# Token weights turned by DMA transposes instead of TensorE, and a reordered first batch, in a fused attention and token-mixing kernel

## The chip, the cores and the metric

The kernel runs on one core of one Trainium2 chip. The metric is device time in microseconds, the median of several executions.

Engine names in the profile: PE is TensorE's matmuls and PEld its weight loads, DVE is VectorE, ACT is ScalarE, POOL is GpSimd (it issues the loads from memory here) and SP is SyncE (it issues the DMA transposes and the stores).

## The reference, cut to what matters

Four batches, eight heads, 768 tokens, head size 64, so a model width of 512.

```python
# attention: local window of 96 tokens plus 8 global ones, with a slope per head
scores = scale * q @ k.T + bias                      # (4, 8, 768, 768)
a = softmax(where(keep, scores, -1e9));  x = a @ v   # -> (4, 768, 512)
# phase mixing of tokens
theta = x @ w_theta                                  # (512, 512)
zr, zi = x * cos(theta), x * sin(theta)
u = x + w_tok_r @ zr + w_tok_i @ zi                  # w_tok_*: (768, 768), on the token axis
out = u + relu(u @ w_ch)                             # (512, 512)
```

The kernel's token mix takes the token weights with the summed token on the partitions, so both `w_tok` matrices are transposed once: 72 blocks of 128 by 128.

## The kernel before

The four batches are software-pipelined. While batch b is mixed (theta, sines, token mix, channel product), the attention of batch b+1 runs beside it. The first batch's attention has nothing beside it and is ordered by hand.

The loads go through one queue on GpSimd, in the order in which they are issued, and convert float32 to bfloat16 on the way:

```python
    load_w()            # w_theta, six loads of w_tok (two row blocks of one matrix each), w_ch
    load_all_qk(1)      # q and k of batch 1
    load_all_v(1)
    load_all_qk(2)
    ...                 # v of batch 2 and half of batch 3's q, k: later, from the stage's step list
```

The token weights are transposed on TensorE, six blocks at a time, and copied from PSUM:

```python
    def trans_w(tt, copy=nc.vector.tensor_copy):
        for wi in range(2):
            ps = ps_small([T, NT, T], BF)
            for st in range(NT):
                nc.tensor.transpose(ps[:, st, :], w_nat[wi, tt][:, st * T:(st + 1) * T], ident)
            (copy if wi else nc.vector.tensor_copy)(out=w_tokT[wi][:, :, tt * T:(tt + 1) * T], in_=ps)
```

`trans_w(0)` stands in the first batch's tail. The other five are woven into batch 0's mixing stage, one ahead of each token row block.

q and k are transposed on TensorE as well. Two heads share one 128-wide transpose, which needs the heads side by side in memory, so VectorE rearranges first:

```python
    def prep_copy(b, p):                       # rearranging copies, two per pair of heads
        ...
            for i_ in range(2):
                nc.vector.tensor_copy(out=qkn[:, :, i_].rearrange("p t h d -> p h t d"),
                                      in_=qk[:, i_, 2 * p:2 * p + 2])

    def prep(b, p):
        ...
                for t_ in range(NT):
                    nc.tensor.transpose(ps[:, t_, :], qkn[:, t_, i_].rearrange("p h d -> p (h d)"), ident)
```

The first batch's tail, in order of issue:

```python
    values(0, NP - 1, 0)
    values(0, NP - 1, 1)          # last pair of heads, all six token blocks
    trans_w(0, nc.scalar.copy)
    xtrans(0, NP - 1)             # x of the last pair, transposed
    for c in range(NT // 2):      # theta of two token blocks at a time, all four pairs
        theta(0, c, 0)
        theta(0, c, 1)
```

For batches 1 to 3 the transposes of x and u are DMA transposes from SyncE. `prep(1, *)` and `prep(2, *)` both run in batch 0's mixing stage. Batch 3's q and k are transposed by DMA.

The softmax here doesn't subtract the row's maximum and nothing guards it: scores larger than these inputs give would overflow.

Of the kernel before, what the change touches and what calls it, by code (L numbers as in the profile page):

```python
# [9 lines left out]
FP = mybir.dt.float32  # L10
# [6 lines left out]
def kernel(  # L17
# [90 lines left out]
    load_qk(0, 2, 2)  # L108
    load_v(0, 0, 4)
    load_qk(0, 4, 2)  # L110
# [29 lines left out]
    def bias_table(p):  # L140
        for h in (2 * p, 2 * p + 1):
            nc.scalar.activation(etab[:, h], dist[:, 0:5], AF.Exp, scale=-slopes[h])  # L142
# [8 lines left out]
    w_nat = {}  # L151
    w_tokT = [const.tile([T, NT, S], BF, name=f"w_tokT_{wi}") for wi in range(2)]

    def load_w():
        nc.gpsimd.dma_start(out=w_theta_bf, in_=moe_w_theta.rearrange("(c p) n -> p c n", p=T))
        for tt in range(0, NT, 2):
            for wi, src in enumerate((moe_w_tok_r, moe_w_tok_i)):
                w2 = moe.tile([T, 2, S], BF, name="w_nat", bufs=6)
                nc.gpsimd.dma_start(
                    out=w2, in_=src[tt * T:(tt + 2) * T, :].rearrange("(a p) s -> p a s", p=T))  # L160
                w_nat[wi, tt], w_nat[wi, tt + 1] = w2[:, 0], w2[:, 1]
        nc.gpsimd.dma_start(out=w_ch_bf, in_=moe_w_ch.rearrange("(c p) n -> p c n", p=T))

    def trans_w(tt, copy=nc.vector.tensor_copy):
        for wi in range(2):
            ps = ps_small([T, NT, T], BF)
            for st in range(NT):
                nc.tensor.transpose(ps[:, st, :], w_nat[wi, tt][:, st * T:(st + 1) * T], ident)
            (copy if wi else nc.vector.tensor_copy)(out=w_tokT[wi][:, :, tt * T:(tt + 1) * T], in_=ps)


# [21 lines left out]
    def cast0(p, i_, eng, h=None):  # L193
        if (p, "n") not in tiles0:
            tiles0[p, "n"] = att.tile([T, NT, 2, 2, D], BF, name="qkn", bufs=2)
        src = qk32[:, i_] if p == 0 else loads[0][0][:, i_, 2 * p:2 * p + 2]
        hs = slice(0, 2) if h is None else slice(h, h + 1)
        eng(out=tiles0[p, "n"][:, :, i_, hs].rearrange("p t h d -> p h t d"), in_=src[:, hs])

    def turn0(p, i_):  # L200
        qkn = tiles0[p, "n"]
        ps = tiles0[p, i_] = ps_small([T, NT, T], BF)
        for t_ in range(NT):
            nc.tensor.transpose(ps[:, t_, :], qkn[:, t_, i_].rearrange("p h d -> p (h d)"), ident)
# [9 lines left out]
    def kglob(b, p):  # L214
        kT = qkT[(b, p)][1]
        kG = qkT[(b, p)][2] = att.tile([T, NT - 2, T], BF, name="kG", bufs=6)
        with behind("dve") if b == B - 1 else nullcontext():
            nc.vector.tensor_copy(  # L218
                out=kG, in_=kT[:, T:(NT - 1) * T].rearrange("p (t n) -> p t n", t=NT - 2))
            nc.vector.tensor_copy(out=kG[:, :, 0:NG], in_=kT[:, None, 0:NG].to_broadcast([T, NT - 2, NG]))  # L220

    qkns = {}

    def prep_copy(b, p):
        qk = loads[b][0]
        qkn = qkns[b, p] = att.tile([T, NT, 2, 2, D], BF, name="qkn", bufs=2)
        with behind("dve"):
            for i_ in range(2):
                nc.vector.tensor_copy(  # L229
                    out=qkn[:, :, i_].rearrange("p t h d -> p h t d"), in_=qk[:, i_, 2 * p:2 * p + 2])  # L230

    def prep(b, p):
        if p == 0:
            prep_copy(b, 0)
        if p + 1 < NP:
            prep_copy(b, p + 1)
        qkn = qkns[b, p]
        qT = att.tile([T, S], BF, name="qT", bufs=6)
        kT = att.tile([T, S], BF, name="kT", bufs=6)
        for i_, dst in ((0, qT), (1, kT)):  # L240
            ps = ps_small([T, NT, T], BF)
            with behind("pe"):
                for t_ in range(NT):
                    nc.tensor.transpose(ps[:, t_, :], qkn[:, t_, i_].rearrange("p h d -> p (h d)"), ident)  # L244

            dst = dst.rearrange("p (n t) -> p n t", t=NT)
            src = ps.rearrange("p t n -> p n t")
            if i_ == 0:
                nc.vector.tensor_copy(out=dst, in_=src)
            else:  # L250
                nc.scalar.copy(out=dst, in_=src)

        qkT[(b, p)] = [qT, kT, None]
        kglob(b, p)
# [42 lines left out]

    def score_exp(b, p, c):
# [4 lines left out]
        if c == NT // 2 - 1 and p == NP - 1:  # L303

            with tc.issue_after(ins) if b else nullcontext():
                nc.scalar.activation(junk, halfpi, AF.Sin)
# [29 lines left out]
    def values(b, p, hh):  # L336
# [9 lines left out]
        for it in range(NT):  # L346
            mms = [(e_t[:, hh, it, 0, :], vn[:, h, it, :])]
            if it:
                mms.append((e_t[:, hh, it - 1, 1, :], vG[:, h, it - 2, :] if it > 1 else vn[:, h, 0, :]))
            o = po[:, 0, it * (D + 1):(it + 1) * (D + 1)]  # L350
            for i_, (l_, r_) in enumerate(mms):
                nc.tensor.matmul(o, lhsT=l_, rhs=r_, start=(i_ == 0), stop=(i_ == len(mms) - 1))  # L352
# [5 lines left out]
        po4 = po[:, :, 0:NT * (D + 1)].rearrange("p a (t d) -> p a t d", d=D + 1)  # L358
        rec = att.tile([T, n, NT, 1], FP, name="rec", tag=f"rec{n}")
        nc.vector.reciprocal(rec, po4[:, :, :, D:D + 1])  # L360
        xv = x_sb[b][:, p, :, h0 * D:(h0 + n) * D].rearrange("p t (a d) -> p a t d", a=n)
        nc.vector.tensor_mul(xv, po4[:, :, :, 0:D], rec.to_broadcast([T, n, NT, D]))  # L362

    def xtrans(b, p, copy=nc.vector.tensor_copy):
# [6 lines left out]
        for st in range(NT):  # L371
            nc.tensor.transpose(ps[:, st * T:(st + 1) * T], x_sb[b][:, p, st, :], ident)
        copy(out=xT_sb[b][:, p, :], in_=ps)
# [4 lines left out]
    def theta(b, c, j):  # L378
        if c == 0 and j == 0:
            zri[b] = moe.tile([T, 2, NT, DM], BF, name="zri", tag="zri", bufs=1)  # L380
        xT, xb = xT_sb[b], x_sb[b]
        last = c == NT // 2 - 1
        if j == 0:
            pss["th"] = [ps_small([T, DM], FP) for _ in range(2)] if last else ps_big()
        pb = pss["th"]
        st = lambda j_: slice((2 * c + j_) * T, (2 * c + j_ + 1) * T)
        for j_, dc in ([(0, dc) for dc in range(NC - 1)] if j == 0 else
                       [(1, dc) for dc in range(NC - 1)] + [(0, NC - 1), (1, NC - 1)]):
            nc.tensor.matmul(pb[j_] if last else pb[:, j_, :], lhsT=xT[:, dc, st(j_)],  # L389
                             rhs=w_theta_bf[:, dc, :], start=(dc == 0), stop=(dc == NC - 1))  # L390
        if j == 1:
# [11 lines left out]
    def mix(b, tt, g):  # L403
# [3 lines left out]
        for st in (2 * g, 2 * g + 1):  # L407
            for wi in range(2):
                anchor["pe"] = nc.tensor.matmul(  # L409
                    ps, lhsT=w_tokT[wi][:, st, tt * T:(tt + 1) * T], rhs=zri[b][:, wi, st, :],  # L410
# [43 lines left out]
    gate = const.tile([1, 1], BF)  # L454

# [6 lines left out]
    def attention_steps(b, preps):  # L462
# [3 lines left out]
        add(0, alloc_x, b)  # L466
        chunks = [(p, c) for p in range(NP) for c in range(NT // 2)]
# [3 lines left out]
        for i_ in range(0, len(chunks), 2):  # L471
# [3 lines left out]
            if b == B - 1 and i_ in (0, 2, 6):  # L475
                add(0, kglob, b, (1, 2, 0, 3)[i_ // 2])
            if i_ == 8:
# [26 lines left out]
    load_w()  # L504
    load_all_qk(1)
    load_all_v(1)
# [6 lines left out]
    cast0(0, 1, dve, 0)  # L513
    cast0(0, 1, act, 1)
    turn0(0, 1)
    cast0(0, 0, dve, 0)
    cast0(0, 0, act, 1)
    turn0(0, 0)
    out0(0, 1, act, 0)
# [3 lines left out]
    kglob(0, 0)  # L523
    score_bias(0, 0)
    score_bias(0, 1)
    score_mms(0, 0, 0)
    score_mms(0, 0, 1)
    score_exp(0, 0, 0)
    cast0(1, 1, dve)
    cast0(1, 0, dve)  # L530
    diagonals(1)
    turn0(1, 1)
    turn0(1, 0)
    for p in range(NP):
        nxt = p + 1 < NP
        score_exp(0, p, 1)
        if nxt:
            out0(p + 1, 1, act)
            out0(p + 1, 0, dve)
            kglob(0, p + 1)  # L540
# [3 lines left out]
        score_bias(p, 2)  # L544
        score_mms(0, p, 2)
        score_exp(0, p, 2)
        if p + 2 < NP:
            cast0(p + 2, 1, dve)
            cast0(p + 2, 0, dve)
            diagonals(p + 2)  # L550
        if p == 0:
            vglob(0, 0, 4)
        if p == 1:
            vglob(0, 4, 4)
        if nxt:
            score_bias(p + 1, 0)
            score_mms(0, p + 1, 0)
            score_exp(0, p + 1, 0)
            score_bias(p + 1, 1)
            score_mms(0, p + 1, 1)  # L560
            if p + 2 < NP:
                turn0(p + 2, 1)
                turn0(p + 2, 0)
        if p:
            xtrans(0, p - 1, act if p == NP - 1 else dve)
    values(0, NP - 1, 0)
    values(0, NP - 1, 1)
    trans_w(0, nc.scalar.copy)
    xtrans(0, NP - 1)
    for c in range(NT // 2):  # L570
        theta(0, c, 0)
        theta(0, c, 1)
    for p in range(NP):
        bias_table(p)
# [5 lines left out]
    for b in range(B):  # L580
# [4 lines left out]
        ahead = [[lambda p=p: prep(2, p) for p in range(NP)], [lambda p=p: prep_dma(3, p) for p in range(1)],  # L585
# [9 lines left out]
        for tt in range(NT):  # L595
            for g in range(NT // 2):
                if (b, tt) != (B - 1, NT - 1):
                    main.append((2048, lambda tt=tt, g=g: mix(b, tt, g)))
                if b == 0 and g == 1 and tt + 1 < NT:
                    main.append((1536, lambda tt=tt: trans_w(tt + 1)))  # L600
# [59 lines left out]
```

## Time and profile before

175.32 us, median of 3 runs (175.06 to 175.37). The profiled execution spans 172.6 us.

These are rows of the page's second part: the span in 40 slices of 4.3 us, busy tenths for the engines, granted clock, busy share of the 16 DMA engines, and GB/s. The last line is the chain of waits by engine.

```profile
PE   6479979999999999999999998999999989999991
DVE  7678965678999999999587588597786837724443
PEclk9999999999999999999999999999999999999998
DMA  5999999999999999879999997787138571323335
...
PE 59%; DVE 21%; ACT 10%; DMA 6%; issue 1%; SPq 0%; DVEq 0%; ACTq 0%
```

Counting slices from 1, TensorE is full from slice 7 on. The DMA row reads 9 until slice 16, about 70 us. VectorE is full from slice 11 to 19.

Marks from the trace: first exp of the first batch at 9.32 us, its last exp ends at 25.30, first sine at 29.91, first token mix at 33.17. The last product of z ends at 36.45 us for batch 0, 81.31 for batch 1, 116.15 for batch 2 and 149.75 for batch 3. I use these four marks to say in which stage time is lost.

### The profile page before, as it was taken

How to read it: one execution, taken by the hardware profiler on the slowest of the kernel's cores; microseconds unless marked ns; L12 is line 12 of the kernel's file. 1: busy time of each engine (PE TensorE's matmuls, PEld its weight loads, DVE VectorE, ACT ScalarE, POOL GpSimd, SP SyncE). 2: the span in 40 equal slices, each digit the busy share in tenths (PEclk: the TensorE clock that was granted, in tenths of full speed). 3: DMA queues.
4: the chain of work that ended last, by engine and by line, in shares of the span. 5: the costliest groups of instructions: out<-in, count | busy, mean ns of one | idle time of the engine just before them, and what ended most of it. 6: DMA issues, size and time to landing. Idle time of an engine off the chain costs nothing.

```text
span 172.6 us, 3652 instructions
## 1 busy us (share of the span) xinstructions
PE 159.9 (93%) x1482; PEld 83.5 (48%) x1482; DVE 128.5 (74%) x288; ACT 99.1 (57%) x124; POOL 37.9 (22%) x45
## 2 busy tenths in 40 slices
PE   6479979999999999999999998999999989999991
PEld 1245655455756566544455463444554634444440
DVE  7678965678999999999587588597786837724443
ACT  2479676999497595489834740979348308500010
POOL 8974355005272010099300000000000000000000
PEclk9999999999999999999999999999999999999998
DMA  5999999999999999879999997787138571323335
GB/s 146 192 193 178 210 208 209 204 204 171 160 204 175 166 155 128 132 97 154 210 141 80 224 158 165 138 152 226 30 76 113 135 171 40 142 41 102 100 93 182
DMA packets 75088, 25.92 MB, mean 150 GB/s; under 512 B 63168, under 2 KB 72128, under 8 KB 75072
## 3 DMA queue, kind: packets, MB, share of 16 engines
q0 software_dynamic: 45680, 12.45, 78.4%
q1 hardware_dynamic: 28976, 12.72, 36.6%
q10 hardware_dynamic: 416, 0.52, 0.9%
q8 instruction: 11, 0.18, 0.4%
q14 instruction: 5, 0.04, 0.1%
HBM read 25.69 MB, written 6.29 MB: 185 GB/s over the span
## 4 chain that ended last, share of the span: by engine, by line
PE 59%; DVE 21%; ACT 10%; DMA 6%; issue 1%; SPq 0%; DVEq 0%; ACTq 0%
PE ps L409 29%; PE ps L434 10%; PE pb L389 5%; PE pb L295 4%; PE pb L352 4%; DVE x_sb L362 4%; ACT etab L142 3%; PE ps L389 3%; ACT e L302 3%; DMA qk<-in_k_dram 3%; DVE kG L218 2%; DVE e L312 2%; ACT cs L395 2%; DMA kT<-qk 2%; DMA xT<-x_sb 2%; PE ps L244 2%
## 5 line engine op out<-in xcount | busy, mean ns | idle before, releaser
L409 PE MATMUL ps<-zri,w_tokT 128*128 128x512 bf16 x288 | 70.6, 380 | 0.3 <-DVE o_sb L440 0.2
L302 ACT ACTIVATE e<-pb 128x1024 bf16<-128x1024 f32 (+1 forms) x48 | 43.6, 958 | 23.1 <-PE pb L295 22.9
L409 PEld LDWEIGHTS <-w_tokT 128*128 128x128 bf16 x288 | 26.1, 98 | 29.0 <-issue 1.0
L414 DVE TENSOR_TENSOR u<-x_sb,ps 128x512 bf16<-128x512 bf16 x24 | 16.4, 682 | 14.6 <-PE ps L409 14.6
L434 PE MATMUL ps<-w_ch_bf,uT 128*128 128x512 bf16 x96 | 24.2, 379 | 0.0
L398 DVE TENSOR_TENSOR zri<-x_sb,cs 128x512 bf16<-128x512 bf16 x48 | 17.9, 418 | 8.0 <-ACT cs L395 7.8
L440 DVE SCALAR_TENSOR_TENSOR o_sb<-ps,u 128x512 f32<-128x512 f32 (+1 forms) x25 | 16.5, 662 | 3.1 <-PE ps L434 3.1
L395 ACT ACTIVATE cs<-pb,halfpi 128x1024 bf16<-128x1024 f32 x8 | 8.9, 1116 | 15.7 <-PE pb L389 15.7
L312 DVE TENSOR_TENSOR e<-e,etab 128x1024 bf16<-128x1024 bf16 (+1 forms) x24 | 14.7, 615 | 3.4 <-ACT e L302 3.4
L389 PE MATMUL pb<-w_theta_bf,xT 128*128 128x512 bf16 x64 | 15.2, 379 | 1.0 <-DMA xT<-x_sb 1.0
L295 PE MATMUL pb<-qT,kT 64*128 64x128 bf16 x224 | 15.6, 219 | 0.6 <-DVE qT L211 0.3
L295 PEld LDWEIGHTS <-kT 64*128 64x128 bf16 x224 | 9.0, 94 | 14.1 <-issue 12.5
L389 PEld LDWEIGHTS <-xT 128*128 128x128 bf16 x96 | 9.0, 98 | 12.0 <-DMA xT<-x_sb 2.4
L428 ACT COPY uT<-ps 128x512 bf16<-128x512 bf16 x7 | 4.1, 587 | 18.6 <-PE ps L427 18.6
L352 PEld LDWEIGHTS <-e 128*128 128x128 bf16 x352 | 12.7, 97 | 3.3 <-issue 1.5
L434 PEld LDWEIGHTS <-uT 128*128 128x128 bf16 x96 | 8.9, 98 | 10.0 <-ACT uT L428 0.3
L295 PE MATMUL pb<-qT,kG 64*128 64x128 bf16 x128 | 11.7, 217 | 1.2 <-DVE kG L220 1.2
L88 POOL DMA_DIRECT2D vn<-in_v_dram x5 | 9.7, 1930 | 12.2 <-DVE vn L68 10.6
L362 DVE TENSOR_TENSOR x_sb<-pb,rec 128x768 bf16<-128x768 f32 x12 | 11.4, 949 | 0.3
L315 DVE TENSOR_TENSOR e<-e,etab 128x1024 bf16<-128x1024 bf16 x12 | 8.2, 684 | 2.8 <-ACT e L302 2.8
L352 PE MATMUL pb<-vn,e 128*128 128x65 bf16 x168 | 9.6, 193 | 0.3 <-DVE x_sb L362 0.3
L82 POOL DMA_DIRECT2D qk<-in_q_dram x8 | 7.4, 920 | 8.8 <-DVE qkn L229 5.0
(74 smaller groups left out, 203.0 us busy)
## 6 DMA issues: line engine op xcount, KB each, us to landing
out_dram<-o_sb SPq DMA_DIRECT2D x23, 256.0 KB, 2.4
vn<-in_v_dram POOLq DMA_DIRECT2D x3, 768.0 KB, 22.7
qk<-in_q_dram POOLq DMA_DIRECT2D x2, 768.0 KB, 21.0
qk<-in_k_dram POOLq DMA_DIRECT2D x2, 768.0 KB, 23.6
w_nat<-in_moe_w_tok_r_dram POOLq DMA_DIRECT2D x3, 384.0 KB, 13.7
w_nat<-in_moe_w_tok_i_dram POOLq DMA_DIRECT2D x3, 384.0 KB, 14.6
vn<-in_v_dram POOLq DMA_DIRECT2D x2, 384.0 KB, 8.9
qk<-in_q_dram POOLq DMA_DIRECT2D x8, 96.0 KB, 9.7
```

The source lines that it names most:

```text
L295: nc.tensor.matmul(pb[:, hh, o:o + T], lhsT=lhsT, rhs=qT[R, (own, nxt)[part]], start=bool(b), stop=bool(b) or (jt == NT - 1 or (j == 1 and ...
L302: ins = nc.scalar.activation(e_c, pb[:, :, 0:n], AF.Exp, scale=scale).ins
L312: nc.vector.tensor_mul(e_c, e_c, tab[:, :, s0:s0 + n // T].rearrange("p a s n -> p a (s n)"))
L352: nc.tensor.matmul(o, lhsT=l_, rhs=r_, start=(i_ == 0), stop=(i_ == len(mms) - 1))
L362: nc.vector.tensor_mul(xv, po4[:, :, :, 0:D], rec.to_broadcast([T, n, NT, D]))
L389: nc.tensor.matmul(pb[j_] if last else pb[:, j_, :], lhsT=xT[:, dc, st(j_)], rhs=w_theta_bf[:, dc, :], start=(dc == 0), stop=(dc == NC - 1))
L395: nc.scalar.activation(o, p_, AF.Sin, **bias)
L398: nc.vector.tensor_mul(zri[b][:, i_, 2 * c + j_, :].rearrange("p (g d) -> p g d", g=NP), xb[:, :, 2 * c + j_, :], cs[:, i_, j_].rearrange( ...
L409: anchor["pe"] = nc.tensor.matmul(ps, lhsT=w_tokT[wi][:, st, tt * T:(tt + 1) * T], rhs=zri[b][:, wi, st, :], start=(st == 0 and wi == 0), ...
L414: anchor["dve"] = nc.vector.tensor_add(u_sb[b, tt].rearrange("p (g d) -> p g d", g=NP), x_sb[b][:, :, tt, :], ps.rearrange("p (g d) -> p g ...
L434: nc.tensor.matmul(ps_c, lhsT=uT[:, dc, :], rhs=w_ch_bf[:, dc, :], start=(dc == 0), stop=(dc == NC - 1))
L440: nc.vector.scalar_tensor_tensor(o_sb[:, cols], in0=ps_c[:, cols], scalar=0.0, in1=u[:, cols], op0=ALU.max, op1=ALU.add)
```

## The change

The intent is to take work off TensorE and VectorE in the stage where both are busy, and to reach the first theta earlier.

1. Token weights: no `trans_w`. Each load of weights (384 KB) is followed by a DMA transpose from SyncE into `w_tokT`. A gate stands behind each pair of weight loads: a tiny GpSimd copy that reads the pair's second tile, so that the loads issued after it start only when the pair has landed. The order of the loads changes so that keys of batch 1 come before the third pair.
2. Column tiles: q and k are transposed one head at a time, 64 columns wide, into one half of the PSUM tile's partitions. The rearranging copies fall away.
3. First batch: theta of the first three pairs goes ahead of the last pair, which is done in two token pieces. Score biases, bias tables and copies move.
4. Half of batch 2's q and k preparation moves from batch 0's stage into batch 1's.

```diff
+    def after_load(tile):
+        return nc.gpsimd.tensor_copy(out=gate, in_=tile[0:1, 0, 0:1]).ins
+
+    def load_w_tok(tt):
+        for wi, src in enumerate((moe_w_tok_r, moe_w_tok_i)):
+            w2 = moe.tile([T, 2, S], BF, name="w_nat", bufs=6)
+            nc.gpsimd.dma_start(
+                out=w2, in_=src[tt * T:(tt + 2) * T, :].rearrange("(a p) s -> p a s", p=T))
+            nc.sync.dma_start_transpose(
+                out=w_tokT[wi][:, tt:tt + 2].rearrange("p a s t -> p (a s) t"),
+                in_=w2.rearrange("p a s -> p (a s)"))
+        return w2
...
+    def turn(ps, src):
+        for t_ in range(NT):
+            for hh in range(2):
+                nc.tensor.transpose(ps[hh * D:(hh + 1) * D, t_, :], src[:, hh, t_, :], ident)
...
-    def prep_copy(b, p):            # and its calls
...
-    load_w()
+    nc.gpsimd.dma_start(out=w_theta_bf, in_=moe_w_theta.rearrange("(c p) n -> p c n", p=T))
+    after_load(load_w_tok(0))
+    after_load(load_w_tok(2))
     load_all_qk(1)
+    after_load(load_w_tok(4))
+    nc.gpsimd.dma_start(out=w_ch_bf, in_=moe_w_ch.rearrange("(c p) n -> p c n", p=T))
     load_all_v(1)
     load_all_qk(2)
...
-    values(0, NP - 1, 0)
-    values(0, NP - 1, 1)
-    trans_w(0, nc.scalar.copy)
-    xtrans(0, NP - 1)
-    for c in range(NT // 2):
-        theta(0, c, 0)
-        theta(0, c, 1)
+    values(0, p, 0, 0, 4)           # p = NP - 1: last pair, token blocks 0 to 3
+    values(0, p, 1, 0, 4)
+    xtrans(0, p - 1, act)
+    sine_table()
+    theta(0, 0, 2)                  # blocks 0 and 1, first three pairs
+    xtrans(0, p, dve, 0, 4)
+    values(0, p, 0, 4, 6)
+    values(0, p, 1, 4, 6)
+    theta(0, 1, 2)
+    theta(0, 0, 3)                  # blocks 0 and 1, last pair: then its sines
+    xtrans(0, p, dve, 4, 6)
+    theta(0, 1, 3)
+    theta(0, 2, 2)
+    theta(0, 2, 3)
...
-        ahead = [[lambda p=p: prep(2, p) for p in range(NP)], ...
+        ahead = [[lambda p=p: prep(2, p) for p in range(NP // 2)], ...
...
-                if b == 0 and g == 1 and tt + 1 < NT:
-                    main.append((1536, lambda tt=tt: trans_w(tt + 1)))
```

## The prediction

> **What bounds the kernel now.** Span 172.6 us. The chain of waits is 59% TensorE, 21% VectorE, 10% ScalarE. By stage (windows, timeline, chain):
> - 0 to 28 us, attention of the first batch: ScalarE and VectorE in turns; TensorE works about 15 us of it. First exp at 9.32 us, last at 25.3, theta products from 28.15, first sine at 29.91, first token mix at 33.17.
> - 42 to 61 us: VectorE is 99 to 100% busy (7.54 of 7.60 us, 11.0 of 11.0), TensorE's queue follows it. 61 to 80: TensorE again; first mix of batch 1 at 80.36.
> - 80 to 105: TensorE (24.9 of 25.0 us). Afterwards nothing that the change touches.
> - Loads: the DMA row is 9 in every slice to 70 us, at about 206 GB/s. Token weights land at 21.6, 23.4, 25.3, 27.3, 29.1, 31.0 us, keys of batch 1 at 41.3, its values at 48.05. The first transposes of batch 1 start at 41.7, on their heels.
>
> **Removed.** 72 TensorE transposes of token weights, 12 in 0.67 us: 4.0 us, 3.3 of it after 33 us; 11 VectorE copies (0.45 us each on the chain, about 5) and one ScalarE copy. All 22 rearranging copies of q and k (16 of 0.27 us and 6 of 0.3): about 4.5 us of VectorE from 41 us on, 1.8 before.
>
> **Added.** Twice as many q/k transposes, half as wide. The Trainium skill (TensorEngine Tiling, Restrictions and Gotchas) says that column tiling excludes fast weight load, yet may run two tiles at once. Row tiles in this trace do (16 score matmuls in 0.55 us). Estimate: 12 take 0.40 us where 6 took 0.34; at worst 0.67. Plus six DMA transposes of 384 KB. "TRN2 transpose DMAs are as fast as regular DMAs" (Advanced Engine Details and Errata, X-Bar Transpose); here a 192 KB one lands 1.55 us after its issue when alone, but took 8.7 us from its issue beside loads at 57 us. At the best packet rate seen, one of 384 KB is 1.5 us of all engines: 9 us in all. Three gates on the load queue add gaps, which the transposes partly fill.
>
> **Moved.** Half of batch 2's q/k preparation goes from the VectorE-bound stage into the TensorE-bound one: about 1.5 to 2.5 us lost there. Theta of three pairs goes ahead, the last pair in two pieces: first sine near 27 (-3 us).
>
> **On the critical path.** VectorE loses about 11 us of work between 41 and 75 us, so TensorE could finish batch 0's stage 5 to 6 us earlier, if data were there. But keys of batch 1 land no earlier (41 to 43), so the 3 us of the first stage are mostly spent waiting; values of batch 1 slip from 48 to 54 or later, and VectorE's copy of them stands ahead of the score multiplications. I expect half or more of the gain to be given back there.
>
> **Time:** 173.0 us, 167 to 180 eight times in 10. Chances: faster 0.38, same 0.42, slower 0.20.
>
> **What would show it.** Right: first sine near 27 us; no rearranging copies; new TensorE or VectorE waits on a DMA (keys, token weights or values of batch 1) between 34 and 60 us; VectorE below 90% from 42 to 61. Wrong: values of batch 1 landing before 50 us (then 168 to 170), or after 58 (then 178 or more); 12 column-tile transposes above 0.6 us.
>
> **What would make it wrong.** DMA transposes that hardly disturb the loads, or starve beside them; column tiles that do not overlap; late transposes of x for batch 1 behind the longer load queue.

## More of the kernel before

The next lines are busy times by stretch, in us from the span's start. The columns are the stretch and its length, then PE, PEld, DVE, ACT and POOL busy time with instruction counts, then granted clock, the mean DMA share (the time that packets took, over the stretch; it exceeds 1 where their times overlap) and GB/s.

```profile
36.00:42.00 6.00, 5.94 (x44) 2.99 (x42) 4.40 (x11) 5.98 (x9) 2.21 (x1) 1.00 1.68 189
42.00:50.00 8.00, 7.83 (x96) 5.40 (x94) 7.94 (x20) 5.64 (x9) 3.28 (x5) 1.00 2.42 173
50.00:60.00 10.00, 9.56 (x130) 5.37 (x128) 10.00 (x21) 7.26 (x9) 2.46 (x3) 1.00 2.37 177
60.00:68.00 8.00, 7.68 (x116) 5.16 (x115) 8.00 (x19) 6.20 (x8) 0.83 (x1) 1.00 2.13 137
68.00:74.00 6.00, 5.99 (x50) 3.35 (x48) 6.00 (x16) 2.20 (x4) 0.39 (x2) 1.00 1.08 161
74.00:82.00 8.00, 8.00 (x54) 3.79 (x53) 7.67 (x20) 7.80 (x10) 8.00 (x9) 1.00 1.22 110
```

From 36 to 82 us VectorE is busy 44.0 of 46.0 us, and TensorE 45.0. Both are full.

## The result, and the profile after

The changed kernel takes 196.28 us (196.01 to 197.99, 4 runs); the kernel before in the same rounds takes 175.34 (175.06 to 176.01). The ratio is 1.121, with a 95% interval of 1.114 to 1.128. It is slower by 12%, far outside the predicted range.

The same rows of the page, after (slices of 4.9 us, as the span is 194.5 us):

```profile
PE   7589987922964759996999999979999998999991
DVE  5656865511370197895668887748687782843442
PEclk9889999985695766999999999999999999999999
DMA  5999999999999999999999977877824545232424
...
PE 48%; DMA 32%; POOL 7%; DVE 7%; issue 2%; ACT 1%; SPq 1%; DVEq 0%; POOLq 0%; ACTq 0%
```

The chain of waits went from 6% DMA to 32%. TensorE and VectorE have holes in slices 9 to 15 (39 to 73 us), and the granted clock falls there.

These are the longest wait of the whole program on GpSimd and VectorE's longest wait for a transfer, then TensorE's four longest waits on transfers from 33 to 101 us. The columns are engine, tile and line, what it waited for, us in total, number of times, longest.

```profile
POOL gate L155 <- DMA w_nat<-in_moe_w_tok_i_dram: 36.3, 3, 14.3
DVE vG L317 <- DMA vn<-in_v_dram: 10.4, 2, 10.0
...
PE ps L424 <- DMA w_ch_bf<-in_moe_w_ch_dram: 4.1, 1, 4.1
PE ps L196 <- DMA qk<-in_k_dram: 3.0, 1, 3.0
PE ps L196 <- DMA qk<-in_q_dram: 2.5, 1, 2.5
PE ps L399 <- DMA w_tokT<-w_nat: 1.9, 1, 1.9
```

TensorE waits on every kind of load: channel weights, keys, queries and transposed weights. VectorE waits 10 us for the values of batch 1. GpSimd, which only issues loads, stands at the three gates for 36 us. Waiting at a gate is harmless in itself. What matters is what it does to the queue behind it, and the landing times tell that. I worked this table out from the trace's records of each transfer (us from the span's start; a pair's two tiles are separated by a slash).

| transfer | before | after |
|---|---|---|
| weights, pair 1 | 21.6 / 23.4 | 22.0 / 25.0 |
| weights, pair 2 | 25.3 / 27.3 | 32.6 / 35.1 |
| weights, pair 3 | 29.1 / 31.0 | 50.0 / 52.3 |
| their DMA transposes | none | 26.3 / 32.8, 36.6 / 41.0, 54.1 / 59.5 |
| channel weights | 33.5 | 60.9 |
| q / k of batch 1 | 37.4 / 41.3 | 44.3 / 48.2 |
| v of batch 1 | 48.05 | 67.11 |
| last transpose of x, batch 1 | 73.5 | 92.1 |

Where the 21.9 us of the profiled spans (194.5 minus 172.6) arise, by the marks of z: 18.8 us by the end of batch 1's z (100.08 against 81.31), another 2.65 from there to batch 2's (37.49 against 34.84), nothing from there to batch 3's (33.64 against 33.60), and 0.4 in the tail. The 18.8 us are close to the 19.1 us by which batch 1's values are late, but the link runs through the transposes of x: batch 1's x is finished 17.6 us late (88.02 against 70.39), its last transpose lands 18.6 us late, and z ends 8.0 us after that landing (7.8 before).

That last landing is the mark to watch in the experiments. In 12 of the 17 kernels with a trace, batch 1's z ends 7.8 to 8.5 us after it, in the other five 9.4 to 9.9. d1 below brings the values forward and not this landing, and gains nothing.

The first stage gained nothing. Its last z ends at 36.35 us, against 36.45.

### The profile page after: what moved, and what is told of

Its sections match the earlier page's. It is cut to its first block, busy times and chain, and to the rows that moved or that the text cites. A ratio compares the mean times of both kernels' runs of the same rounds, so it can differ in the third digit from the quotient of the medians.

```text
span 194.5 us, 3753 instructions
## 1 busy us (share of the span) xinstructions
PE 162.9 (84%) x1529; PEld 82.0 (42%) x1554; DVE 118.2 (61%) x258; ACT 100.1 (51%) x127; POOL 37.8 (19%) x48
## 4 chain that ended last, share of the span: by engine, by line
PE 48%; DMA 32%; POOL 7%; DVE 7%; issue 2%; ACT 1%; SPq 1%; DVEq 0%; POOLq 0%; ACTq 0%
PE ps L399 26%; DMA w_nat<-in_moe_w_tok_i_dram 20%; PE ps L424 7%; DMA vn<-in_v_dram 7%; PE pb L277 4%; DMA xT<-x_sb 4%; PE pb L336 4%; POOL qk L73 3%; PE pb L379 3%; PE ps L379 2%; POOL vn L88 1%; DMA kT<-qk 1%; DVE o_sb L430 1%; PE ps L196 1%; DVE zri L388 1%
## 5 line engine op out<-in xcount | busy, mean ns | idle before, releaser
L399 PE MATMUL ps<-zri,w_tokT 128*128 128x512 bf16 x273 | 71.6, 393 | 3.6 <-DMA w_tokT<-w_nat 1.9
L287 ACT ACTIVATE e<-pb 128x1024 bf16<-128x1024 f32 (+1 forms) x48 | 44.2, 953 | 31.3 <-PE pb L277 30.6
L277 PE MATMUL pb<-qT,kT 64*128 64x128 bf16 x224 | 16.3, 231 | 1.9 <-DVE qT L207 1.3
L196 PE MATMUL ps<-ident,qk 128*64 128x128 bf16 x288 | 12.5, 244 | 6.3 <-DMA qk<-in_k_dram 3.0
L336 PEld LDWEIGHTS <-e 128*128 128x128 bf16 x352 | 13.3, 99 | 8.1 <-DVE e L296 2.9
L277 PEld LDWEIGHTS <-kT 64*128 64x128 bf16 x224 | 9.0, 98 | 17.6 <-issue 14.1
L231 DVE COPY qT<-ps 128x768 bf16<-128x768 bf16 x8 | 7.6, 952 | 12.9 <-PE ps L196 12.9
L196 PEld LDWEIGHTS <-qk 128*64 128x64 bf16 x288 | 10.1, 124 | 11.2 <-issue 3.6
L336 PE MATMUL pb<-vn,e 128*128 128x65 bf16 x168 | 10.5, 197 | 3.8 <-DVE e L296 2.5
L277 PE MATMUL pb<-qT,kG 64*128 64x128 bf16 x128 | 12.4, 231 | 0.4 <-DVE kG L218 0.4
L233 ACT COPY kT<-ps 128x768 bf16<-128x768 bf16 x8 | 6.4, 799 | 11.0 <-PE ps L196 10.9
## 6 DMA issues: line engine op xcount, KB each, us to landing
qk<-in_k_dram POOLq DMA_DIRECT2D x2, 768.0 KB, 14.6
```

Of the source, the lines that this page charges most:

```text
L196: nc.tensor.transpose(ps[hh * D:(hh + 1) * D, t_, :], src[:, hh, t_, :], ident)
L277: nc.tensor.matmul(pb[:, hh, o:o + T], lhsT=lhsT, rhs=qT[R, (own, nxt)[part]], start=bool(b), stop=bool(b) or (jt == NT - 1 or (j == 1 and ...
L287: ins = nc.scalar.activation(e_c, pb[:, :, 0:n], AF.Exp, scale=scale).ins
L336: nc.tensor.matmul(o, lhsT=l_, rhs=r_, start=(i_ == 0), stop=(i_ == len(mms) - 1))
L399: anchor["pe"] = nc.tensor.matmul(ps, lhsT=w_tokT[wi][:, tt, st, :], rhs=zri[b][:, wi, st, :], start=(st == 0 and wi == 0), stop=(st == NT ...
```

## The experiments

### Which part of the weights' path costs what: a1, a2, a3, b1

Theory A says that the queue of loads is what got slower, through the transposes' traffic and the gates, and a1 to a3 split the two. Theory B, the rival, says that the cost lies in the rest of the change.

a1 is the changed kernel with the weights transposed on TensorE again, no gates, and the loads in the order of before:

```diff
-            nc.sync.dma_start_transpose(out=w_tokT[wi][:, tt:tt + 2]..., in_=w2...)
+    def trans_w(tt, copy=nc.vector.tensor_copy): ...    # as before; trans_w(0) ahead of sine_table()
-    after_load(load_w_tok(0))
-    after_load(load_w_tok(2))
-    load_all_qk(1)
-    after_load(load_w_tok(4))
-    (w_ch)
+    load_w_tok(0); load_w_tok(2); load_w_tok(4); (w_ch); load_all_qk(1)
```

> The changed kernel with one part undone: token weights transposed on TensorE as before (72 transposes, 12 copies, all on VectorE), loads in the order of before, no gates. The other two parts stay (first batch reordered, column-tile transposes). Theory A (the token-weight part alone costs the 21 us): values of batch 1 land near 48 us again, no VectorE wait on them, 165 to 174 us. Rival B (the new first batch or the column-tile transposes cost it, and the slow clock with them): stays above 183 us.

a2 is a1 with the changed kernel's order of loads and its three gates. No DMA transpose of weights is in it.

> As a1_pe_weights, and the same instruction order on TensorE, but with the changed kernel's load order and its three gates on the load queue; no DMA transposes. Theory A1 (the transposes' own traffic is what delays the loads): three gaps of 2 to 3 us, values of batch 1 land at 54 to 58 us, 173 to 179 us. Rival A2 (the gates delay them): values land after 63 us, 188 us or more.

a3 is the changed kernel with its DMA transposes, without gates, and the loads in the order of before.

> The changed kernel with its DMA transposes, loads in the order of before and no gates. A1 (traffic): the transposes go beside a full load queue and the values of batch 1 still land 9 to 14 us late (57 to 62), 182 to 195 us; the first token mix also waits for its transposed weights. A2 (gates): values land before 52 us, below 174 us.

b1 is a1 plus the six DMA transposes of weights, written to a tile that nobody reads.

> As a1_pe_weights, plus the six DMA transposes of 384 KB into a tile that nobody reads; ungated. Only their traffic is added, nothing waits for them. A1 (traffic): against a1 the values of batch 1 land 9 to 12 us later (57 to 60 us) and the time rises by 5 to 10 us. Rival A3 (the traffic fits in beside the loads and the cost is the wait for the transposed weights): values within 3 us of a1, time within 1.5 us of a1.

| kernel | weights by | gates | us (range, 4 runs) | ratio, 95% | v of batch 1 lands |
|---|---|---|---|---|---|
| before | TensorE | no | 174.62 (174.35 to 176.10, 7 runs) | | 48.05 |
| a1 | TensorE | no | 176.71 (176.58 to 177.27) | 1.010 (1.005 to 1.016) | 47.83 |
| a2 | TensorE | yes | 191.31 (189.65 to 194.06) | 1.091 (1.081 to 1.100) | 58.16 |
| a3 | DMA | no | 195.06 (194.51 to 195.41) | 1.115 (1.109 to 1.121) | 63.56 |
| b1 | TensorE, and DMA unread | no | 196.14 (195.64 to 197.35) | 1.123 (1.116 to 1.129) | 53.46 |
| changed | DMA | yes | 196.28 (196.01 to 197.99), own rounds | 1.121 (1.114 to 1.128) | 67.11 |

Nearly all of the loss is in the weights' path, and theory B falls: a1 keeps everything else of the change but the order of the loads and is at +1%. The gates alone (a2 less a1) delay batch 1's values by 10.3 us, 3.4 us for each gate. The transposes on top (changed less a2) delay them by another 9.0 us. My expectation for a2 (173 to 179 us) was a miss. I had taken the gates for cheap. a3 came out just past the upper ends of its expectation (62 us for the values, 195 us).

The new order of loads is not what delays the values in a2: c2 below has the same order without gates, and they land at 48.28.

The stretches 22 to 25 and 28 to 33 us show what a gate does. The lines are a1, then a2, then the changed kernel, with the columns as above:

```profile
22.00:25.00 3.00, 2.92 (x60) 2.01 (x58) 2.65 (x8) 2.40 (x3) 1.38 (x2) 1.00 1.16 209
28.00:33.00 5.00, 3.72 (x22) 1.58 (x19) 2.85 (x11) 3.15 (x5) 0.68 (x1) 1.00 1.21 206
```

```profile
22.00:25.00 3.00, 2.92 (x60) 2.01 (x58) 2.65 (x8) 2.41 (x3) 1.61 (x3) 1.00 0.24 30
28.00:33.00 5.00, 3.72 (x22) 1.57 (x19) 2.85 (x11) 3.15 (x5) 2.25 (x4) 1.00 0.52 79
```

```profile
22.00:25.00 3.00, 2.93 (x60) 2.01 (x58) 2.65 (x8) 2.41 (x3) 0.00 (x0) 1.00 0.81 88
28.00:33.00 5.00, 3.72 (x21) 1.58 (x18) 2.85 (x11) 3.19 (x5) 0.00 (x0) 1.00 1.08 170
42.00:50.00 8.00, 2.63 (x27) 1.65 (x28) 0.96 (x1) 0.96 (x2) 0.00 (x0) 0.51 1.26 206
```

In a1 206 to 209 GB/s are moved in these two stretches, in a2 30, then 79. A gate lets the queue run dry: the pair must land, the copy must run, the next load must be issued, and its first packets must start. In a2 the last load packet before the first gate starts at 22.75 us, the gate opens at 23.28, the next load is issued at 23.51, its first packet starts at 24.93, and the full rate is back after 26. The Trainium skill (SBUF — State Buffer, The DMA setup-cost knee) puts a roughly fixed cost of 2 us on every transfer, mostly for its completion. My reading is that a gate takes that cost out of hiding. This trace agrees on the size: 2.2 us pass between the last packet before the first gate and the first one after it, and 2.7 and 2.5 at the other two. It does not agree on the division: of the 2.2 us, 0.5 lie before the gate opens and 1.4 between the next issue and its first packet. The whole price is 3.4 us a gate.

Do the transposes fill those gaps? I counted the packets that start in each microsecond. Loads of weights have packets of 1536 bytes, the transposes of 256. (The 35 in the last line of a2 are the keys' first, of 768 bytes.)

```
us      a2: load   changed: load  changed: transpose
22          35           32            0
23           0            5          477
24           7            1          234
25          40            0          825
26         106            0          557
27         129            0          639
28         138           56          331
29          92          109            9
30           0          109            0
31           0          121            0
32          35          103            0
```

In the changed kernel the transposes run in the gap, but the gap becomes longer for it: the load queue is back at 29 us instead of 26. The second tile of the pair, on which the gate waits, also lands later (25.0 us instead of 23.2), because the transpose of the first tile is already under way. So the two costs add up. The prediction had them overlap in part.

Leaving the gates out does not help. In a3 the load queue is never dry, and the six transposes starve. This is SyncE's issuing of them, and TensorE's wait for the result:

```profile
22.15 36.53 SPq L162 DMA_TRANSPOSE w_tokT<-w_nat  x6
```

```profile
PE ps L399 <- DMA w_tokT<-w_nat: 14.4, 3, 8.7
```

Six issues take 36.5 us, and TensorE waits 14.4 us for transposed weights. The first transpose lands at 38.1 us, 16 us after its issue began, and the last at 68.9. The values of batch 1 land 15.7 us later than in a1 (63.56 against 47.83), with no gate at all. So the gates have a purpose: they get the transposes through. Both ways cost about 20 us against the kernel before. In time the two costs do not add: over a1, gates alone cost 14.6 us (a2), transposes alone 18.4 (a3), both 19.6 (the changed kernel, other rounds).

In b1 the result of the transposes isn't needed, and yet the time is that of the changed kernel. These are TensorE's longest wait there, and SyncE's:

```profile
PE pb L389 <- DMA xT<-x_sb: 12.5, 3, 10.5
SPq L165 <- DMA unread<-w_nat: 40.8, 5, 10.5
```

The second line is a fault of the test. All six transposes write one tile with a single buffer (`bufs=1`), so each is issued only when the one before has landed, and SyncE stands 40.8 us at that. The transposes of x of batch 1 are behind them in SyncE's order: x is finished at 74.34 us, its last transpose is issued at 87.84. b1 was expected at +5 to +10 us over a1 and came out at +19, but from the end of x to the landing of its last transpose it takes 16.3 us where a1 takes 3.1, so much of the loss is this queueing, and b1 does not show what the transposes' traffic costs. It shows that their traffic delays the loads even when nobody needs the result: the values land 5.6 us later than in a1 (outside both branches of the expectation), batch 2's keys 10.0 us later (64.82 against 54.80), and x of batch 1 is finished 5.5 us later. A run with a buffer for each transpose would have been the clean test, and it was not made.

The granted clock falls as well. In the last line of the changed kernel above, TensorE works 2.63 of 8 us and its granted clock is 0.51. The Trainium skill (TensorE: Matmul & The Clock Gate, What's actually happening) calls throttled the default state, to which an idle engine returns. The trace agrees: token mix products that take 379 ns take 607 to 634 ns there. What the lower clock costs in all was not measured apart.

### Can the values be brought forward: d1

If the delay of batch 1's values alone were the loss (theory V), another order of loads would win part of it back. d1 is the changed kernel with the loads in the order weights 1, gate, weights 2, gate, q and k of batch 1, channel weights, v of batch 1, weights 3, gate, q and k of batch 2:

```diff
     load_all_qk(1)
-    after_load(load_w_tok(4))
     nc.gpsimd.dma_start(out=w_ch_bf, ...)
     load_all_v(1)
+    after_load(load_w_tok(4))
     load_all_qk(2)
```

> The changed kernel, DMA transposes and three gates kept, same TensorE order; only the loads are reordered: channel weights and values of batch 1 go ahead of the third pair of token-weight tiles. Theory V (the late values of batch 1, landing at 67.1 us, are what the stage ends on): values land at 56 to 59 us and the time falls by 6 to 10 us to 186 to 190. Rival (the transposed weights themselves, or the slow clock, set the time): less than 3 us gained.

197.93 us (197.83 to 198.05), ratio 1.131 (1.127 to 1.135). The values land at 56.4 us instead of 67.1, and VectorE no longer waits for them. TensorE's waits are now for keys and queries, those of batch 2 standing behind the third gate (7.6 and 5.6 us in all), and for the third pair of weights (3.4 us). The longest:

```profile
PE ps L196 <- DMA qk<-in_k_dram: 7.6, 2, 4.6
```

Theory V falls. The first two pairs of batch 1 are 11 us earlier than in the changed kernel (x of the first at 62.95 us against 73.83), but the third is finished at 84.27, the last transpose of x lands at 92.55 (92.09 in the changed kernel), and z ends at 101.08. Everything in the queue is late, and the order only chooses which consumer waits.

### Why the rest of the change gains nothing: c1, c2, c3

a1 keeps the column tiles, the new first stage and the moved preparation, and is 1% slower than before. Three steps follow. c1 is a1 with the preparation of batch 2 back in batch 0's stage (`late = []`, `range(NP)`). c2 is c1 with q and k of batch 1 loaded ahead of the third pair of weights. c3 is c2 with the tail reordered:

```diff
     xtrans(0, p - 1, act)
+    values(0, p, 0, 4, 6)
+    values(0, p, 1, 4, 6)
-    trans_w(0)
+    trans_w(0, act)
     sine_table()
-    theta(0, 0, 2)
     xtrans(0, p, dve, 0, 4)
-    values(0, p, 0, 4, 6)
-    values(0, p, 1, 4, 6)
-    theta(0, 1, 2)
-    theta(0, 0, 3)
+    theta(0, 0, 2)
     xtrans(0, p, dve, 4, 6)
+    theta(0, 0, 3)
+    theta(0, 1, 2)
```

> a1_pe_weights with the q/k preparation of batch 2 wholly back in batch 0's stage, as before. Between the last phase product of batch 1 and that of batch 2, a1 took 37.6 us and the kernel before 34.8. Theory P (the moved half of the preparation lengthens the TensorE-bound stage): that stretch is back within 0.5 us of 34.8, the batch-0 stage grows by at most 1.5 us, total 1 to 2.5 us below a1 (174 to 175.5). Rival (something else in that stage, such as slower column-tile transposes disturbing the score products): the stretch stays above 36.5 us.

> c1_prep_back with keys and queries of batch 1 loaded ahead of the third pair of token-weight tiles (the changed kernel's load order, without its gates); the instruction order of TensorE is the same. If the wait for these keys (landing at 41.6 us in a1) bounds the start of batch 1, they land near 35.5 us and the time falls by 1 to 3 us. If VectorE bounds the rest of that stage, nothing is gained (within 0.7 us of c1).

> c2_keys_first with the tail of batch 0 reordered: the last pair's transposes of x go ahead of theta, and theta's last product for the first two token tiles directly behind their first three. Theory O (the new order gained nothing because TensorE's queue stood at a theta product that waits for ScalarE's copy, with the finished last pair behind it): the first sine starts at 28.5 to 29.0 us in place of 29.85, and the last phase product of batch 0 1 us earlier than 36.4. Rival (ScalarE or VectorE alone bound the tail): first sine after 29.5 us.

| kernel | us (range, 6 runs) | ratio, 95% |
|---|---|---|
| before, same rounds | 174.81 (174.37 to 175.87, 11 runs) | |
| c1 | 177.02 (176.11 to 177.38) | 1.011 (1.008 to 1.014) |
| c2 | 176.89 (176.01 to 177.27) | 1.010 (1.007 to 1.013) |
| c3 | 177.00 (176.30 to 177.83) | 1.011 (1.008 to 1.015) |

No step gains or loses anything. c1, expected 1 to 2 us below a1, shifts 1.9 us from the stretch between batch 1 and 2 (35.7 us instead of 37.6) into batch 0's stage (z of batch 1 ends at 81.85 us instead of 79.93) and is neutral. c2 brings the keys of batch 1 forward from 41.9 to 35.7 us, and nothing uses it. c3 was to bring the first sine to 28.5 to 29.0 us. It comes at 29.68, in the range of the rival.

One caution for such marks: a1, c1, c2 and e1 (below) have the same order of instructions for the first batch, and its last exp ends at 25.25, 25.58, 24.74 and 25.56 us. A difference of under 1 us at such a mark between single profiles lies within this scatter.

To see why the prediction's "first sine near 27" failed, look at the tail of the first batch in the changed kernel. These are timeline lines, with the columns start in us, duration in us, engine, line, operation, tiles, count, and in brackets what the engine waited for:

```profile
24.44 0.81 ACT L287 ACTIVATE e<-pb 128x768 bf16<-128x768 f32 x1 [0.59 <-PE pb L277]
...
25.69 0.80 ACT L359 COPY xT<-ps 128x768 bf16<-128x768 bf16 x1 [0.45 <-PE ps L358]
...
26.55 1.04 PE L379 MATMUL pb<-w_theta_bf,xT 128*128 128x512 bf16 x4 [0.68 <-ACT xT L359]
27.42 0.39 PE L358 MATMUL ps<-ident,x_sb 128*128 128x128 bf16 x4
...
27.89 1.89 PE L379 MATMUL pb<-w_theta_bf,xT 128*128 128x512 bf16 x8
...
29.82 1.11 ACT L385 ACTIVATE cs<-pb,halfpi 128x1024 bf16<-128x1024 f32 x1 [1.81 <-PE pb L379]
```

The last exp ends at 25.25 us (25.30 before). TensorE's queue stands at the theta products that were to fill the time, until ScalarE's copy of the third pair is done (26.55). The last pair's x transposes stand behind those (27.42). Then come eight theta products, 1.9 us (27.89): six of the next two blocks, and only then the two of the last pair that the first sine needs. It starts as they end (29.82). What was to run in the shadow of the last pair runs in front of it. From the last exp's end to the first sine it is 4.57 us, against 4.61 before.

c3 takes the second obstacle away and gets 4.38 us. There another one stands in its place: ScalarE copies transposed weights first, and then the load of its sine table occupies it until just before the first sine.

```profile
27.46 0.80 ACT L172 COPY w_tokT<-ps 128x768 bf16<-128x768 bf16 x1 [0.92 <-PE ps L171]
...
28.28 1.28 ACT L288 ACT_TABLE_LOAD   x1
...
29.68 1.10 ACT L392 ACTIVATE cs<-pb,halfpi 128x1024 bf16<-128x1024 f32 x1
```

So c3 tests the order only in part: I put that copy there myself. What the best order would give stays open.

### A transpose of x, the column tiles alone, and one more order: e1, e2, f1, e3

In c2 the transposes of x of batch 1 take longer to land than before. Theory L says that they eat what VectorE gains, because the loads of batch 3's q and k are in flight beside them. e1 is c2 with those loads moved behind batch 1's last transpose, e2 is the kernel before with the same move:

```diff
         with tc.issue_after(g):
-            load_qk_tokens(b, H // 2, H // 2)
+            load_qk_tokens(b, 0, H)
...
-            side.append((0, lambda: (alloc_qk(3), load_qk_tokens(3, 0, H // 2))))
+            side.append((0, lambda: alloc_qk(3)))
```

f1 is the kernel before with the column tiles and nothing else: `turn` in place of the wide transposes, no rearranging copies. e3 is e1 with c3's tail and `score_mms(0, 0, 1)` ahead of `turn0(1, *)`.

> c2_keys_first with one move: the first half of the loads of batch 3's q and k (16 transfers, in c2 in flight between 62 and 70 us) goes behind the gate on the last transpose of x of batch 1. Theory L (the shorter VectorE work of c2 lets the last transpose of x of batch 1 issue at 64.4 us instead of 70.4, but beside those loads it takes 8.6 us to land, so the first theta product of batch 1 still waits until 73.1): without the loads it lands in about 3 us, near 68; last zri of batch 1 at 77 to 79 instead of 81.7; the time 172 to 174, faster than the kernel before by about 1%. Rival theory N (the transpose is slow for another reason, the load of batch 2's values at 62 to 63 us or the output stores): it still takes 6 us or more and the time stays at 176 to 177. Rival theory S (batch 3's keys then come too late for batch 3's scores): new waits on q and k after 110 us, 177 or more.

> The kernel before with the same move of batch 3's loads, nothing else. There the last transpose of x of batch 1 issues at 70.4 us, when the loads have nearly ended, and lands in 3.1 us. Theory L: next to nothing, 174.3 to 175.3. Theory S: 177 or more. If this gains as much as e1, the gain of e1 belongs to the move alone, and not to what the column tiles freed.

> The kernel before with the column-tile transposes alone: no rearranging copies, same loads, same order of the first batch, weights on TensorE. If c1's 1% is a cost of the new order of the first batch (bias table of head 0 early, theta of three pairs ahead, the last pair in two pieces), this is at 174 to 175; if it is the column tiles (24 transposes in 0.80 us where 12 took 0.67, which lengthens TensorE's queue at 61 to 80 us, and the loads of batch 3 beside the transposes of x as in theory L), it is at 176 to 177 like c1.

> e1 with the first batch's tail in the order of c3 and the score products of the first pair's second chunk put ahead of the second pair's transposes. Those products should bring the second exp from 10.8 to about 10.3 us, and each later exp of the first stage by up to 0.5 us if ScalarE bounds there; last exp 24.9 to 25.3, first sine 29.2 to 29.7. The time is that of e1 or up to 0.5 us less. If it is more than 0.5 us slower than e1, the order harms.

| kernel | us (range, 4 runs) | ratio, 95% |
|---|---|---|
| before, same rounds | 174.61 (174.30 to 175.80, 7 runs) | |
| e1 | 177.10 (176.09 to 179.16) | 1.012 (1.007 to 1.017) |
| e2 | 179.78 (178.75 to 180.48) | 1.029 (1.024 to 1.033) |
| f1 | 177.14 (176.60 to 178.55) | 1.015 (1.010 to 1.020) |
| e3 | 177.36 (175.99 to 178.18) | 1.017 (1.013 to 1.021) |

Theory L rested partly on a misreading, which its expectation repeats: 64.4 us is the issue of the third of four transposes in c2, not of the last. The last is issued at 68.2 us in c2 (70.4 before) and lands at 73.7 (73.5 before). So 2.2 us gained at the issue are lost in flight. In e1 the last one is issued at 68.9 and lands at 72.0, in 3.1 us as theory L wanted, and it does not help: batch 1's z ends at 81.69 us, as in c2 (81.71). TensorE has become the limit there, busy 6.00 of 6.00 us from 68 to 74. Theory L falls as the explanation of the time. e2 shows the price of the moved loads in the next stage, where TensorE waits 4.6 us for transposes of x of batch 2. In e3 the second exp ends at 10.53 us instead of 10.85 in e1, but the last ends at 24.90, within the scatter named above, and the time is unchanged.

f1 settles one thing: the column tiles alone, on the kernel before, are as slow as a1, c1 and c2. The new first stage is not needed to explain the 1%. It is not that column tiles are slow on TensorE: 24 of them, undisturbed, take 0.86 us, where 12 wide transposes took 0.83 to 0.84. Here is f1 from 36 to 60 us, stretch by stretch:

```profile
36.00:42.00 6.00, 5.70 (x48) 2.85 (x46) 3.79 (x9) 5.99 (x9) 2.21 (x1) 1.00 1.68 188
42.00:50.00 8.00, 7.83 (x135) 5.12 (x135) 7.18 (x16) 5.61 (x9) 2.31 (x3) 1.00 2.36 175
50.00:60.00 10.00, 9.21 (x145) 5.67 (x143) 9.94 (x20) 7.19 (x9) 4.23 (x5) 1.00 2.04 180
```

VectorE is relieved mostly before 50 us (11.0 us busy from 36 on, instead of 12.3). From 50 to 60, after the values of batch 1 have landed at 48.2, it is as full as before (9.94 of 10), and TensorE stays at 44.6 of the 46 us to 82. My reading is that what is saved ahead of that landing waits for it; this is argued, not shown. Its last x of batch 1 is finished 1.3 us earlier than before's (69.06 us against 70.39), but the transpose takes 4.9 us from issue to landing instead of 3.1 and lands 0.5 us later, as in c2. What exactly makes f1 2 us slower (0.9 us from batch 0's z to batch 1's, 1.0 from there to batch 2's) I did not find, and it stays open.

### What free weights would have been worth: h1, h2; and column tiles only where TensorE has room: g1

New theory T: TensorE bounds the stage, and VectorE's relief is idle. Then the weights' transposes, taken off TensorE at no cost in transfers, should pay. h1 is a1, and h2 is c2, with the weights loaded by ordinary transfers straight into the place of their transposes and never transposed. The result is wrong (relative error 0.96), and it is the ceiling of what a DMA path for the weights could bring in this kernel:

```diff
-            w2 = moe.tile([T, 2, S], BF, name="w_nat", bufs=6)
-            nc.gpsimd.dma_start(out=w2, in_=src[tt * T:(tt + 2) * T, :]...)
+            nc.gpsimd.dma_start(out=w_tokT[wi][:, tt:tt + 2].rearrange("p a s t -> p a (s t)"), in_=src[...]...)
-    def trans_w(...)        # and its calls
```

g1 is c2 with e3's order of the first batch; the column tiles stay in the first batch, while `prep` has the rearranging copies and wide transposes of before.

> a1 with the token weights loaded straight into the place of their transposes, by ordinary transfers, and never transposed: a wrong result on purpose, and the ceiling of what the change's transfer by DMA could have brought if it cost nothing. Theory T (TensorE bounds from 36 us on): the 60 transposes after 33 us are 3.3 us of TensorE, so 172.5 to 174.0 against 176.7 of a1. Rival theory V (VectorE bounds 42 to 61 us, as the prediction had it, and it is relieved of 10 more copies, 4.5 us): 171 to 172.5. Rival theory D (the landing of batch 1's values and keys bounds): 175.5 or more.

> c2 (keys first, preparation of batch 2 wholly in the first stage) with the same free weights, wrong result on purpose. Theory T: like h1 or up to 1 us less, since moving half of the preparation only moves TensorE work from one full stage to another: 172 to 174. If the move paid (h2 more than 1 us slower than h1), the place of the preparation mattered once TensorE was relieved.

> e1's and e3's order of the first batch with column tiles for the first batch alone; q and k of batches 1 and 2 go through the rearranging copies and wide transposes of the kernel before; weights on TensorE, loads keys first, batch 3's loads as before. Theory T: column tiles cost TensorE time (24 in 0.86 us against 12 in 0.83 at most, plus what their longer queue holds up), so without them where TensorE is full the stage from 36 to 82 us is as in the kernel before, and the first stage's 0.5 us stay: 174.0 to 175.2, possibly the fastest of all. If it is 176 to 177 like c2 and f1, the cost of the column tiles arises in the first batch, or the order is to blame.

| kernel | us (range, runs) | ratio, 95% |
|---|---|---|
| before, same rounds | 174.88 (174.31 to 175.75, 10 fast runs) | |
| h1 | 178.14 (176.70 to 179.04, 4) | 1.017 (1.012 to 1.023) |
| h2 | 175.41 (174.70 to 175.93, 4) | 1.002 (0.999 to 1.006) |
| g1 | 176.11 (174.76 to 177.03, 6) | 1.006 (1.002 to 1.011) |

Theory T falls as it was forecast, and this is the most telling result: in both, the branch that came out is nearest to what the expectation of h1 calls theory D, the landings. With the weights' transposes gone and nothing paid for them, the kernel is no faster than before (h2), or slower (h1). The relief is not worth nothing: h2 is at 1.002 where c2, its counterpart with the transposes, was at 1.010 (other rounds). So about 1.4 us come of the 4 us of TensorE work taken out, by the prediction's count. This is TensorE's and VectorE's work in h1, and TensorE's waits from 36 to 82 us:

```profile
36.00:42.00 6.00, 3.81 (x40) 1.96 (x39) 2.33 (x3) 5.41 (x9) 2.21 (x1) 1.00 1.64 190
...
68.00:74.00 6.00, 2.80 (x10) 0.94 (x8) 2.00 (x3) 0.24 (x1) 0.49 (x2) 0.81 1.27 144
```

```profile
PE pb L375 <- DMA xT<-x_sb: 3.2, 1, 3.2
PE ps L192 <- DMA qk<-in_k_dram: 2.2, 1, 2.2
```

TensorE waits 2.2 us for the keys of batch 1, up to 41.7 us, and 3.2 us for a transpose of x, up to 72.1 (from 68 to 74 it works 2.80 of 6 us). (h2, which loads these keys first, has no wait for them and waits 1.9 us for x.) The last transpose of x is issued at 67.95 us and lands at 73.40, as late as before's 73.50. So a third limit stands right behind the other two: the transfers. In every variant without gates or DMA transposes of weights the values of batch 1 land at 48 to 49 us, batch 2's keys at 55 to 56, and the last transpose of x at 71 to 74. In the kernel before, TensorE (45.0 of 46 us) and VectorE (44.0) are full up to that landing, so all three limits lie close together.

h1 and h2 (2.7 us apart, same rounds) differ in two things, the move of half of batch 2's preparation and the place of batch 1's keys. Between the z marks of batch 1 and 2, where only the move counts, h1 takes 37.58 us and h2 35.44. In a1 against c1 the move gave 1.9 us back in batch 0's stage. In h1 that stage is held by the transfers, and it does not.

g1 is the fastest correct variant of the change, 0.6% slower than the kernel before. It was expected at 174.0 to 175.2 and missed that by 0.9 us. Against c2 and f1 it suggests that the column tiles are cheaper where TensorE has room, but its interval touches that of c2, so this is not shown. No version that I ran beats the kernel before.

## Why the prediction was wrong, point by point

- "Three gates on the load queue add gaps, which the transposes partly fill." This is the step that failed. The gates alone delay batch 1's values by 10.3 us (a2), and the transposes add 9.0 us to that instead of hiding in the gaps. That the 9.0 us equal the estimate ("9 us in all") is luck in part: without gates the same six transposes delay the values by 15.7 us (a3 less a1). The gates' price of 3.4 us each had no number in the prediction. Taking the gates out would not have saved it: the transposes alone cost 18.4 us over a1.
- "values of batch 1 slip from 48 to 54 or later". The direction was right, the size was not: 67.1 us. The prediction's own test for this ("after 58 (then 178 or more)") had the right sign and put no size on the loss. d1 shows that everything behind the gates is late.
- "VectorE loses about 11 us of work ..., so TensorE could finish batch 0's stage 5 to 6 us earlier, if data were there." The work did go away, but there was no gain behind it to give back. TensorE itself was busy 45.0 of 46 us, and with its own 3.3 us taken off as well (h1, h2) it waited for transfers at the stage's end. The condition "if data were there" was the right one to write down, and it decided the case.
- "first sine near 27 (-3 us)". It came at 29.82. The theta products that were to run ahead wait for ScalarE's copy, and those of the next blocks stand in front of the last pair's in TensorE's order. The second exp even ends later (11.80 us, 11.26 before). TensorE's granted clock is 0.57 between 8 and 12 us, where it had been 1.0, but e3 has the same clock there and ends its second exp at 10.53, so this is not shown to be the cause.
- "12 take 0.40 us where 6 took 0.34." Right, and on the cautious side: 24 take 0.86 us in the changed kernel and 12 wide ones 0.83 to 0.84 in the kernel before. The lost fast weight load costs little that is visible: a 64-wide weight load takes 110 ns in c2 (median), a 128-wide one 98.
- "about 1.5 to 2.5 us lost there" for the moved preparation. Right: 1.9 us between the z marks of batch 1 and 2, a1 against c1. (The changed kernel's 2.65 us against the kernel before has other causes in it.)
- "new TensorE or VectorE waits on a DMA ... between 34 and 60 us; VectorE below 90% from 42 to 61". Right, though the waits last longer: that for values ends at 67 us.
- "starve beside them" was listed among what would make the prediction wrong. a3 shows just that: 11 to 20 us to land beside a full queue. "Late transposes of x for batch 1" was listed too, and it came true: the last one lands at 92.09 us instead of 73.50. Most of that is not their flight, as the prediction had it ("behind the longer load queue"): x itself is finished 17.6 us late, and the flight adds 1.0.
- Chances: 0.20 for slower by over 2% was too little. A program whose DMA row reads 9 for the first 70 us has no room for 9 us of extra transfers.

## What to carry to other kernels

Before moving work from an engine to the DMA queues, read the DMA row. Where it was full here, the moved work came on top of the loads and delayed every later one. A gate on the load queue cost 3.4 us each time, and the transfers put into its gap lengthened it. When two engines and the queue are all near full in a stage, taking work off one or two of them may bring little (1.4 us for 4 us in h2): test the ceiling with a version that leaves the work out (a wrong result) before building the real one.

## What the Trainium skill lacked or had wrong

- Advanced Engine Details and Errata, X-Bar Transpose (TRN2): "TRN2 transpose DMAs are as fast as regular DMAs" is given without a condition, and the section gives no rate beside loads. Here, from the start of the issue, one of x (192 KB) lands in 2.7 us with no load beside it but in 8.7 us among loads (the kernel before; the prediction's 1.55 us count from the end of the issue). One of 384 KB took 11 to 20 us beside a full queue (a3), of which the issue itself was held for 4 to 9 us.
- DMA: Bandwidth & Descriptors, Rules for kernel authors: "A transpose next to ordinary DMAs needs nothing" is about correctness, which the correct results of these runs confirm. It says nothing of time: a3, with six transposes of 384 KB beside ordinary loads and no gate, is 18.4 us slower than a1.
- SBUF — State Buffer, The DMA setup-cost knee: the roughly fixed 2 us of a transfer are given for one transfer. No page gives the price of making one load wait for another in a queue that would otherwise stay full. It is 3.4 us each here (a2). The section has the fixed cost mostly in the completion; here 0.5 us of the gap lie before the gate opens and 1.4 between the next issue and its first packet.
- TensorEngine Tiling (Array Packing), Restrictions and Gotchas: it lists fast weight load as lost with column tiling, and gives no time for it. Here 24 column-tile transposes take 0.86 us, about as long as the 12 wide ones they replace (0.83 to 0.84).
